# Two attention layers and feed-forwards on one core: two scratch tiles for the masked maxima, one pool of eight PSUM banks, and the order set anew

## The chip, the core and the metric

The kernel runs on one core of a Trainium2 chip. The core has a matrix engine (TensorE; the profile splits it into PE, the matmuls, and PEld, the loads of their weights), VectorE (DVE), ScalarE (ACT), GpSimd (POOL), and queues that issue DMAs (SP's for most of them, ACT's for one kind). The engines run side by side, each takes its own instructions in the order in which they stand, and they wait for each other by semaphores. TensorE writes its results to PSUM, which has eight banks of 512 fp32 values per partition. The metric is device time in microseconds (us) of one launch; the time of a kernel is the median of its runs.

## The reference

Two layers, each of attention A and feed-forward B with a residual and a layer norm, over 2,048 rows of 512 values. Attention has 32 heads of 16 values and takes the rows in 4 segments of 512. Each segment attends causally to itself, reads a memory matrix M that the earlier segments left, and adds to it.

```python
for s in range(4):
    logits = einsum("bhqd,bhkd->bhqk", qs, ks) * scale + mask     # mask: -1e9 above the diagonal
    a_dot  = einsum("bhqk,bhkd->bhqd", softmax(logits), vs)
    a_mem  = einsum("bhld,bhde->bhle", phi(qs), M) / (einsum("bhld,bhd->bhl", phi(qs), z) + 1e-6)
    outs.append(g * a_mem + (1 - g) * a_dot)                      # g = sigmoid(beta), per head
    M, z = M + einsum("bhld,bhle->bhde", phi(ks), vs), z + sum(phi(ks))
x = x + concat(outs) @ wo
x = x + (silu(ln(x) @ w_gate) * (ln(x) @ w_up)) @ w_down          # F = 1792
```

## The kernel before, in words

**Units.** Attention of a layer is cut into 32 units (64 in both layers): 4 segments, 4 groups of 8 heads, and 2 halves of 4 heads each. For every unit the kernel needs the row maxima of the masked logits before it can take exponentials. So each unit has two passes over its scores:

- *Maxima* (`mx_units`): for each of 4 heads, PE fills three banks named pmx (L545): two query tiles in one bank with 256 columns each, then one of 384 columns, then one of 512. DVE goes over each of the four query tiles with one instruction (L552) that adds the mask `amask`, takes the maximum into an accumulator and writes the masked values, which nobody reads, to a scratch tile `junk`. The widths are 128, 256, 384 and 512. In the profile that is CUSTOM_DVE_ANT_0, followed by DVE_READ_ACCUMULATOR2_ANT, which puts the maximum into the tile `mx`; in the order both read ISA. After the four heads PE transposes `mx` (L561), ACT negates it into `nm` (L563), and a DMA from ACT's queue (L564) lays it into a row of the query tile `cq` (in profile and order a tile s), so that the maximum is subtracted by the matmul itself.
- *Scores* (`at_units`): PE fills banks named plt with the transposed scores (L597, two matmuls of 256 columns each, ten tiles per unit), ACT takes exponentials (L603), POOL zeroes what is above the diagonal (L607), and PE multiplies with V into the bank ppv (L624). DVE then transposes the result and divides it: L641, L642, L643, L645, and L658 for every second unit.

Beside the units run the projections of Q, K, V and the output (`mm3`, L283), three products of high and low fp32r halves each; layer norms (L354 to L379); the memory's read and update (L678, L694, L706); and DMAs that lay q and k out by head through DRAM scratch (L493, L494, then `load3`, L518 and L525, into `cq` and `ck`).

**Feed-forward.** Seven chunks of 256 columns; the first is computed directly (`up`, L1005), the rest by `strassen` (L1035) with seven products in place of eight; `down` (L1079) multiplies back, and DVE adds into the residual (L1084).

**Banks.** Every use of PSUM names its bank: plt_0 to plt_2, pmx_0 and pmx_1, ppv, and two called pj, handed out as they become free, for projections and all else. The feed-forward uses the same names.

**Order.** No order is written by hand. Each instruction is an `Op` with an engine, an estimated cost, a priority and its dependences. `issue` (L149) runs through planned time: each engine takes, of what is ready, the instruction of lowest priority value. `LAT` (L43) holds the assumed delays from one engine to the next, `DRAIN` (L40) the change between kinds of matmul. The priorities come from tables: `OFF` for attention (per layer and kind of work), `PRE` for the start, `EP`, `PAIR`, `STEP` and others for the feed-forward. The order in which `issue` takes them is the order in which they stand on the engines, so a wrong estimate shows as a wait on the chip. What waits for what is found anew when the program is built: an instruction that writes a tile waits for those that wrote or read it, on its own engine too.

Of the kernel before, what the change touches and what calls it, by code (L numbers as in the profile page):

```python
# [30 lines left out]
FIN = 17.556  # L31
WQ1 = -21.562
TA, TF = 15.0, 16.7
OFF = ({'qe': (-9.529, 6.646), 'at': (2.962, 3.706), 'mx': (-19.475, -0.147), 'lf': (1.981, -1.419), 'mr': (3.909, 3.093), 'mu': (-9.872, 0.779), 'wo': (3.44, 3.68), 'qk': (5.846, -0.589), 'v': (-0.011, 4.09), 'lp': (17.308, 14.505)},
       {'qe': (10.232, -1.73), 'at': (1.453, 2.403), 'mx': (0.085, 1.514), 'lf': (6.063, -10.056), 'mr': (1.198, 0.041), 'mu': (3.833, -8.363), 'wo': (4.307, -7.535), 'qk': (4.0, -2.887), 'v': (-1.622, 5.91), 'lp': (-0.044, 3.023)})
PRE = {'w1': -20.101, 'w2': 0.722, 'w3': -15.68, 'c': 15.68, 'mb': 7.879, 'lv': 17.87, 'lo': 8.433, 'gate': 15.128, 'v': 10.65, 'dv': 2.669, 'qk1': -14.13, 'mx': 1.541}
EP = {'w': -5.238, 'wn': 8.96, 'ln': -1.878, 'dn': -2.694, 'up': -2.148}
POOL_W = ""
TABLE = 1.28
DRAIN = {("full", "cols"): 0.2, ("cols", "full"): 0.15}  # L40
# [6 lines left out]
    pool=dict(pool=0.14, dve=0.09, pe=0.19, act=0.14, sp=0.07),  # L47
    sp=dict(act=1.2, dve=1.2, pe=1.2, pool=1.2, sp=1.2),
# [3 lines left out]
class Buf:  # L52
    def __init__(self, prog, pool, tag, shape, dtype):
        self.prog, self.pool, self.tag, self.shape, self.dtype = prog, pool, tag, shape, dtype
        self.ops, self.left = [], 0
        self.w, self.r = {}, {}
        self.tile = None
        self.slot = None
        self.prev = None
        if tag not in prog.shared:  # L60
            self.prev = prog.last.get(tag)
            prog.last[tag] = self
# [6 lines left out]
class Op:  # L69
    __slots__ = ("table", "mode", "post", "eng", "cost", "lat", "fn", "prio", "bufs", "succ", "deps", "ready", "need", "wait", "index")  # L70

    def __init__(self, eng, cost, lat, fn, prio, bufs):
        self.eng, self.cost, self.lat, self.fn, self.prio, self.bufs = eng, cost, lat, fn, prio, bufs
        self.mode, self.table, self.post = None, None, 0.0
        self.succ, self.deps, self.ready, self.need, self.wait = [], set(), 0.0, None, 0


class Program:
# [19 lines left out]
    def op(self, eng, cost, fn, reads=(), writes=(), lat=0.0):  # L98
# [38 lines left out]
        for b in touch:  # L137
            assert b.tag in self.shared or self.last[b.tag] is b, f"{b.tag} was given to another buffer"
            b.ops.append(o)
            b.left += 1  # L140
            if b.tag in self.shared:
                o.need = b
# [6 lines left out]
    def issue(self):  # L149
        for b in {id(b): b for o in self.ops for b in o.bufs if b.tag in self.shared}.values():  # L150
# [15 lines left out]
        held = {tag: [] for tag in self.shared}  # L166
        for o in self.ops:
# [3 lines left out]
        while done < len(self.ops):  # L171
            best = None
            for e in engs:
                f, n = fut[e], now[e]
                while True:
# [3 lines left out]
                    if n:  # L179
                        o = n[0][2]  # L180
                        b = o.need
                        if b is not None and b.slot is None:
                            if not free[b.tag]:
                                heapq.heappop(n)
                                held[b.tag].append(o)
                                continue
                            fr = min(free[b.tag])
                            if fr[0] > t[e] + 1e-9:
                                heapq.heappop(n)
                                o.ready = fr[0]  # L190
# [18 lines left out]
            b = o.need  # L209
            if b is not None and b.slot is None:  # L210
                fr = min(free[b.tag])
                free[b.tag].remove(fr)
                b.slot = fr[1]
# [17 lines left out]
            for b in o.bufs:  # L231
                b.left -= 1
                if b.left == 0 and b.slot is not None:
                    free[b.tag].append((end + 0.25, b.slot))
                    for w in held[b.tag]:
# [11 lines left out]
def infini_swiglu(ctx: ExitStack, tc: tile.TileContext, x, wq, wk, wv, wo, beta, wg, wu, wd, out,  # L247
# [8 lines left out]
    P = Program({"pj": 2})  # L256
# [5 lines left out]
    def bank(tag, ring=1):  # L262
        return P.buf(psum, tag, [128, 512], F32, ring)
# [33 lines left out]
    mhalf = sb("mhalf", [128, 1])  # L297
    amask = sb("amask", [128, 512], BF16)
# [98 lines left out]
    def attention(lay, x_in, x_out, slots, T, hook):  # L397
# [134 lines left out]
        def mx_units(u):  # L532
# [4 lines left out]
            def head(p, j):  # L537
                def f():
                    for grp in ((0, 1), (2,), (3,)):
# [9 lines left out]
                        for a, qt in enumerate(grp):  # L549
                            w = 128 * (qt + 1)  # L550
                            junk = sb("junk", [128, 512], BF16)
                            dve(w, lambda a=a, qt=qt, w=w, ps=ps, junk=junk: nc.vector.tensor_tensor_reduce(  # L552
# [186 lines left out]
        if lay == 0:  # L739
# [14 lines left out]
            for t in range(4):  # L754
                ln_fin(0, t, ("plt_0", "plt_1", "plt_2", "ppv")[t])
# [17 lines left out]
        qk_proj(0, 0, "q", "pj" if lay else "pmx_0")  # L773
        qk_proj(0, 0, "k", "pj" if lay else "pmx_1")
# [5 lines left out]
        for t in range(4):  # L780
            at(PRE["v"] + PRE["dv"] * t)
            v_proj(0, t, "pj" if lay else ("plt_0", "plt_1", "plt_2", "ppv")[t])
# [52 lines left out]
    def ffn(base, x_in, x_out, slots, T):  # L835
# [159 lines left out]
        def up(b, fi, ht, early):  # L995
            res = []
            for nm in "gu":
                ps = bank("pj" if early else ("plt_0", "plt_1", "plt_2", "ppv")[nup[0] % 4])
# [18 lines left out]
        def strassen(c, nm, m):  # L1017
# [3 lines left out]
            PX, PY, PZ = [bank(t) for t in (("plt_0", "plt_1", "plt_2") if nm == "g" else ("ppv", "pmx_0", "pmx_1"))]  # L1021
# [214 lines left out]
```

## Time and profile before

| what | value |
|---|---|
| median of 3 runs | 1925.59 us (1921.84 to 1928.22) |
| the profiled execution | 1928.79 us |
| its span, first to last instruction | 1927.1 us |
| mean granted TensorE clock in it | 0.998 |
| DMA | 206.14 MB, 107 GB/s on average |

The span falls into the start (some 48 us), attention of layer 1 (to about 500 us), its feed-forward (to about 1000), attention of layer 2 (to about 1470) and its feed-forward.

How to read a row of the groups: line, engine, operation, what is written <- what is read, the shape, xcount, then after the first bar busy us in total and mean ns of one, then after the second the engine's idle time just before these instructions and who ended it. In a list of waits: who waited <- for whom: us in total, times, longest us. In a timeline: start, duration, engine, line, operation, and in brackets the idle time before it. In a table of windows: the window, its length, busy us of PE, PEld, DVE, ACT and POOL with their instructions, the clock, DMA share and GB/s. PE's ends are modelled, since its matmuls overlap in the array.

### The profile page before, as it was taken

To read this page: it belongs to the slowest core of one execution; us is meant where nothing else is said; L and a number is where in the kernel's file an instruction comes from. 1 tells how busy PE (TensorE), PEld (TensorE's weight loads), DVE (VectorE), ACT (ScalarE), POOL (GpSimd) and SP (SyncE) were. 2 spreads that over 40 slices of the span, in tenths; PEclk is the share of its full clock that TensorE was granted. 3 is DMA by queue.
4 is the path that set the end of the run, shared out by engine and by line. 5 is a ranking of instruction groups with operands and counts; after the bars stand their busy time and mean duration, and the time that the engine had idled before them with its cause. 6 is when DMAs were issued, how large, how long until landed. Compare 5 with 4: busy or idle time off the path is not lost. (4 is left out here: it accounts for less than half of the span.)

```text
span 1927.1 us, 33037 instructions
## 1 busy us (share of the span) xinstructions
PE 1848.0 (96%) x11360; PEld 1448.9 (75%) x11360; DVE 1433.0 (74%) x3834; ACT 884.1 (46%) x1633; POOL 910.1 (47%) x1186
## 2 busy tenths in 40 slices
PE   6899999999999999999999999999999999999999
PEld 5677777776777877788777777777767788877887
DVE  5778778788786669766867768777797856696656
ACT  4455555555634333334435545555455334333331
POOL 5333444434546453746533335443355365546461
PEclk9999999999999999999999999999999999999999
DMA  7534534457131123111364344363561321221121
GB/s 236 137 84 134 147 116 149 127 153 208 39 134 55 44 77 99 55 55 55 105 212 120 102 138 127 101 178 106 161 179 37 132 66 43 84 77 56 44 60 44
DMA packets 126968, 206.14 MB, mean 107 GB/s; under 512 B 14160, under 2 KB 52048, under 8 KB 126800
## 3 DMA queue, kind: packets, MB, share of 16 engines
q1 hardware_dynamic: 124752, 203.49, 35.7%
q8 instruction: 91, 1.49, 0.3%
q10 hardware_dynamic: 2048, 0.53, 0.1%
q14 instruction: 77, 0.63, 0.1%
HBM read 136.34 MB, written 67.11 MB: 106 GB/s over the span
## 5 line engine op out<-in xcount | busy, mean ns | idle before, releaser
L552 DVE CUSTOM_DVE_ANT_0 junk<-pmx,amask 128x128 bf16<-128x128 f32 (+3 forms) x1024 | 495.5, 484 | 98.4 <-PE pmx L545 43.4
L283 PE MATMUL pj<-s,s 128*128 128x512 f32 x1416 | 476.1, 404 | 3.5 <-DVE raw L989 1.4
L1079 PE MATMUL pj<-s,vt 128*128 128x512 f32 x1296 | 405.9, 397 | 3.6 <-DVE s L1084 2.7
L603 ACT ACTIVATE s<-plt 128x512 f32<-128x512 f32 x448 | 255.9, 604 | 202.2 <-PE plt L597 181.9
L1035 PE MATMUL plt<-s,s 128*128 128x512 f32 x1008 | 320.6, 395 | 8.7 <-ACT s L970 4.0
L545 PE MATMUL pmx<-ck,s 127*128 127x256 f32 (+2 forms) x1024 | 301.4, 344 | 20.2 <-DVE mx L552 12.9
L1079 PEld LDWEIGHTS pj<-s,vt 128*128 128x128 f32 x1296 | 242.8, 188 | 67.0 <-DVE s L1084 5.8
L283 PEld LDWEIGHTS pj<-s,s 128*128 128x128 f32 x1416 | 258.8, 189 | 41.5 <-DVE raw L989 2.3
L597 PE MATMUL plt<-s,ck 128*128 128x256 f32 x1280 | 249.3, 288 | 15.0 <-DMA s<-nm 13.7
L1084 DVE TENSOR_TENSOR s<-s,pj 128x512 f32<-128x512 f32 x224 | 152.3, 684 | 141.3 <-PE pj L1079 139.0
L597 PEld LDWEIGHTS plt<-s,ck 128*128 128x128 f32 x1280 | 220.5, 190 | 47.8 <-DMA s<-nm 19.2
L1035 PE MATMUL pmx<-s,s 128*128 128x512 f32 x720 | 242.8, 395 | 0.0
L607 POOL TENSOR_SCALAR_AFFINE_SELECT s<-s 128x512 f32<-128x512 f32 x192 | 129.7, 676 | 233.1 <-ACT s L603 231.8
L1035 PEld LDWEIGHTS plt<-s,s 128*128 128x128 f32 x1008 | 189.2, 188 | 57.2 <-ACT s L970 6.8
L545 PEld LDWEIGHTS pmx<-ck,s 127*128 127x128 f32 x1024 | 177.9, 189 | 71.7 <-DVE mx L552 19.3
L1035 PEld LDWEIGHTS pmx<-s,s 128*128 128x128 f32 x720 | 135.1, 188 | 31.2
L902 POOL TENSOR_TENSOR s<-mem,s 128x512 fp32r<-128x512 f32 x96 | 128.9, 1349 | 0.7 <-ACT s L901 0.7
L1035 PE MATMUL ppv<-s,s 128*128 128x512 f32 x288 | 113.6, 397 | 2.8 <-ACT s L901 2.8
L624 PE MATMUL ppv<-s,vt 128*32 128x384 f32 (+3 forms) x1536 | 115.7, 419 | 0.0
L909 POOL COPY turn<-vt 128x1 f32<-128x1 f32 x20 | 3.7, 185 | 234.0 <-DVE vt L992 234.0
L479 POOL TENSOR_SCALAR s<-raw 128x512 fp32r<-128x512 f32 x64 | 40.6, 634 | 140.3 <-ACT raw L478 137.7
L624 PEld LDWEIGHTS ppv<-s,vt 128*32 128x32 f32 x1536 | 43.4, 109 | 65.1 <-issue 50.5
(201 smaller groups left out, 2981.2 us busy)
## 6 DMA issues: line engine op xcount, KB each, us to landing
s<-scrq SPq DMA_DIRECT2D x128, 192.0 KB, 3.5
ck<-scrk SPq DMA_DIRECT2D x128, 192.0 KB, 4.4
scrq<-s SPq DMA_DIRECT2D x32, 512.0 KB, 4.2
scrk<-s SPq DMA_DIRECT2D x32, 512.0 KB, 3.6
scrq<-s SPq DMA_DIRECT2D x32, 256.0 KB, 2.9
scrk<-s SPq DMA_DIRECT2D x32, 256.0 KB, 2.3
xin<-xmid SPq DMA_DIRECT2D x32, 256.0 KB, 2.7
s<-xmid SPq DMA_DIRECT2D x32, 256.0 KB, 5.4
```

The costliest lines, as they stand in the source:

```text
L283: pe(n, passes, lambda: nc.tensor.matmul(view(ps.ap), lhsT=av(a.ap), rhs=bv(b.ap), start=start, stop=stop), [(a, rk[0]), (b, rk[1])], [ps])
L479: gp(0.59, lambda: nc.gpsimd.tensor_scalar(out=nat.ap[:, a, 0, :], in0=raw.ap, scalar1=1.0, scalar2=0.0, op0=OP.mult, op1=OP.add), [raw], ...
L545: nc.tensor.matmul(ps.ap[:, a * 256:a * 256 + nk], lhsT=cq.ap[0:127, 2 * j + p, qt * 128:(qt + 1) * 128], rhs=ck.ap[0:127, p, 0:nk], start ...
L552: dve(w, lambda a=a, qt=qt, w=w, ps=ps, junk=junk: nc.vector.tensor_tensor_reduce(out=junk.ap[:, :w], in0=ps.ap[:, a * 256:a * 256 + w], i ...
L597: nc.tensor.matmul(ps.ap[:, 256 * p:256 * p + 256], lhsT=ck.ap[:, p, kt * 128:kt * 128 + 128], rhs=cq.ap.rearrange("r (j p) c -> r p j c", ...
L603: act(512, lambda: nc.scalar.activation(view().rearrange("p x i c -> p (x i c)"), ps.ap, AF.Exp, scale=SCALE), [ps], [(Pb, key)], table="exp")
L607: gp(0.593, lambda: nc.gpsimd.affine_select(out=view()[:, 0], in_=view()[:, 0], pattern=[[0, 4], [1, 128]], compare_op=OP.is_ge, fill=0.0, ...
L624: nc.tensor.matmul(ps.ap[32 * i:32 * i + 32, qt * 128:(qt + k) * 128], lhsT=vt.ap[:, kt, VW * hd:VW * hd + 32], rhs=view(k=k)[:, :, idx], ...
L902: gp(n / 400, lambda hi=hi, lo=lo, src=src: nc.gpsimd.tensor_sub(lo(), src(), hi().bitcast(F32)), [read, (wt, (o0, 0))], [(wt, (o0, 1))])
L1035: pe(512, 1, lambda i=i, kc=kc, x=x, buf=buf, view=view: nc.tensor.matmul(ps.ap, lhsT=w.ap[:, o, i, kc], rhs=view(buf.ap, kc), start=(x == 0),
L1079: pe(512, 1, lambda i=i, j=j, fi=fi, x=x, ps=ps, wt=wt, cs=cs: nc.tensor.matmul(ps.ap, lhsT=ht.ap[:, 0:2048].rearrange("p (f a c) -> p f a ...
L1084: dve(512, lambda ps=ps, t=t: nc.vector.tensor_add(xb.ap[:, t, :], xb.ap[:, t, :], ps.ap), [ps, (xb, t)], [(xb, t)])
```

## The change

1. **Two scratch tiles.** `junk` becomes two lasting tiles, junk_0 of 384 and junk_1 of 512 columns; query tiles 0 and 2 write the first, 1 and 3 the second. Each write has a key of its own, so the planner sees no dependence between two maxima. The built program still orders two writers of one tile, so a maximum now waits for the maximum before the last.
2. **One pool of banks.** All eight banks belong to one pool "ps". A use asks for any free bank, under a cap for its class: 3 each for pj, plt, pmx and ppv, 6 for the feed-forward (ff) and 6 for the start (st). In the feed-forward the old names remain as an order of uses, without a fixed bank.
3. **The planner's numbers.** The assumed delays are smaller (PE to ACT 0.20 for 0.29, ACT to PE 0.17 for 0.39, DVE to DVE 0.13 for 0.19), that of a DMA larger (1.9 for 1.2), and all tables of priorities are new. `nm` has one buffer instead of two.

The instructions are the same in kind and number; their order and their banks are not.

```diff
+CAP = {'pj': 3, 'plt': 3, 'pmx': 3, 'ppv': 3, 'ff': 6, 'st': 6}
-WOT = ("pmx_0", "pmx_1", "pj", "pj")
+WOT = ("st", "st", "pj", "pj")
-PAIR, STEP, WAT, TAT = 15.838, 2.488, -12.222, (-12.051, 7.528)
+PAIR, STEP, WAT, TAT = 11.852, 7.441, 15.217, (16.363, 16.627)
...
-    pe=dict(pe=0.01, act=0.29, dve=0.29, sp=0.27),
-    act=dict(act=0.32, dve=0.19, pe=0.39, pool=0.29, sp=0.22),
-    dve=dict(dve=0.19, act=0.19, pe=0.36, pool=0.23, sp=0.17),
...
+    pe=dict(pe=0.01, act=0.2, dve=0.2, pool=0.26, sp=0.19),
+    act=dict(act=0.22, dve=0.13, pe=0.17, pool=0.19, sp=0.15),
+    dve=dict(dve=0.13, act=0.12, pe=0.2, pool=0.17, sp=0.12),
...
-                        b = o.need
-                        if b is not None and b.slot is None:
-                            if not free[b.tag]:
+                        new = [b for b in o.need if b.slot is None]
+                        if new:
+                            tag = new[0].tag
+                            fr = sorted(free[tag])[:len(new)]
+                            if len(fr) < len(new) or not all(turn[b.cls] for b in new):
...
-    P = Program({"pj": 2})
+    P = Program({"ps": 8})
...
     def bank(tag, ring=1):
-        return P.buf(psum, tag, [128, 512], F32, ring)
+        b = P.buf(psum, "ps", [128, 512], F32)
+        b.cls = tag if tag in CAP else "ff"
+        if b.cls == "ff":
+            b.prev = P.last.get(tag)
+            P.last[tag] = b
+        return b
...
+    junks = [sb(f"junk_{i}", [128, 384 + 128 * i], BF16) for i in range(2)]
...
-                            junk = sb("junk", [128, 512], BF16)
-                            dve(w, lambda a=a, qt=qt, w=w, ps=ps, junk=junk: nc.vector.tensor_tensor_reduce(
+                            dve(w, lambda a=a, qt=qt, w=w, ps=ps, junk=junks[qt % 2]: nc.vector.tensor_tensor_reduce(
...
-                                [(ps, a), amask], [junk, (mx, (qt, p, j))])
+                                [(ps, a), amask], [(junks[qt % 2], (lay, u, p, j, qt)), (mx, (qt, p, j))])
...
-                ps, nm = bank("pj"), sb("nm", [16, 128], F32R, ring=2)
+                ps, nm = bank("pj"), sb("nm", [16, 128], F32R)
```

What this makes of the order, at two places. First DVE, where the seventh unit of layer 1 begins its maxima (tile mx_1465 before, mx_1383 now; a read-out of the accumulator is a row that names mx alone; tt, r and Y are the output chain of an earlier unit). Before:

```order
L641 STREAM_TRANSPOSE tt_1397<-ppv 128x512
L552 ISA junk,mx_1265<-pmx_1390,amask 128x512 [waits DVE_49,PE_49]
L552 ISA mx_1265 128x1
L642 RECIPROCAL r_1415<-tt_1397 128x16 [waits DVE_49]
L552 ISA junk,mx_1265<-pmx_1394,amask 128x128 [waits DVE_49,PE_49]
L552 ISA mx_1265 128x1
L643 TENSOR_SCALAR r_1415<-r_1415,gnot 128x16 [waits DVE_49]
L552 ISA junk,mx_1265<-pmx_1394,amask 128x256 [waits DVE_49]
L552 ISA mx_1265 128x1
L645 TENSOR_TENSOR Y<-tt_1397,r_1415 128x16x16 [waits DVE_49]
```

The same place now:

```order
L653 STREAM_TRANSPOSE tt_1337<-ps_1296 128x512
L654 RECIPROCAL r_1345<-tt_1337 128x16 [waits DVE_49]
L655 TENSOR_SCALAR r_1345<-r_1345,gnot 128x16 [waits DVE_49]
L657 TENSOR_TENSOR Y<-tt_1337,r_1345 128x16x16 [waits DVE_49]
L670 STREAM_TRANSPOSE of<-Y 128x512 [waits DVE_49,Pool_49]
L564 ISA junk_439,mx_1383<-ps_1374,amask 128x128 [waits PE_49]
L564 ISA mx_1383 128x1
L564 ISA junk_445,mx_1383<-ps_1374,amask 128x256
L564 ISA mx_1383 128x1
L564 ISA junk_439,mx_1383<-ps_1377,amask 128x384 [waits DVE_49,PE_49]
L564 ISA mx_1383 128x1
```

Before, each step of the chain and a maximum take turns. Now the chain stands in a row, and the maxima stand in a row behind it, on two tiles in turn. Over the whole program 863 of the 1,024 maxima stand right behind a read-out, where 536 did.

Second PE, behind the transpose that closes the maxima of the ninth unit of layer 1 (s_269 and ck_292 are that unit's query and key tiles before, s_232 and ck_251 now; those with ck_98 and ck_90 are the tenth unit's). Before:

```order
L561 MATMUL pj_2036<-ident,mx_1853 16x128
L678 MATMUL pj_2040<-mb_223,phiq_1868 128x136
L545 MATMUL pmx_2048<-ck_98,s_67 128x512
L678 MATMUL pj_2040<-mb_223,phiq_1868 128x136
L678 MATMUL pj_2053<-mb_223,phiq_1868 128x136
L545 MATMUL pmx_2061<-ck_98,s_67 128x256 x2
L678 MATMUL pj_2053<-mb_223,phiq_1868 128x136
L545 MATMUL pmx_2072<-ck_98,s_67 128x384
L545 MATMUL pmx_2081<-ck_98,s_67 128x512
L597 MATMUL plt_2087<-s_269,ck_292 128x256 x2
```

The same place now, the first rows:

```order
L573 MATMUL ps_1853<-ident,mx_1738 16x128
L295 MATMUL ps_1857<-s_1034,s_109 128x512
L609 MATMUL ps_1861<-s_211,ck_222 128x256 x2
L295 MATMUL ps_1857<-s_1034,s_109 128x512
L609 MATMUL ps_1870<-s_211,ck_222 128x256 x2
L295 MATMUL ps_1857<-s_1034,s_109 128x512
```

Before, the unit's own scores (L597) came ten matmuls after the transpose. Now projections (L295) and the unit before it (s_211, ck_222) come first, and the unit's own scores stand 39 matmuls behind. Over all 64 units the median of that distance goes from 34 to 59 matmuls. In the built program 273 fills of the maxima's banks wait for ACT, and 269 fills of the scores' banks for DVE, where none of either did.

More of the change, by code (lines that the diff above doesn't have):

```diff
@@ L166, in issue @@
         held = {tag: [] for tag in self.shared}
+        turn = {c: [0.0] * n for c, n in CAP.items()}
         for o in self.ops:
@@ L208, in issue @@
             heapq.heappop(n)
[L209 to L213, printed above, removed]
+            for b in o.need:
+                if b.slot is None:
+                    fr = min(free[b.tag])
+                    free[b.tag].remove(fr)
+                    b.slot = fr[1]
+                    turn[b.cls].remove(min(turn[b.cls]))
             for b in o.bufs:
@@ L234, in issue @@
                     free[b.tag].append((end + 0.25, b.slot))
+                    turn[b.cls].append(end + 0.25)
                     for w in held[b.tag]:
@@ L1020, in strassen @@
             (h0, l0), (h1, l1) = XT[2 * m], XT[2 * m + 1]
-            PX, PY, PZ = [bank(t) for t in (("plt_0", "plt_1", "plt_2") if nm == "g" else ("ppv", "pmx_0", "pmx_1"))]
+            PX, PY, PZ = [bank(t) for t in (("plt_0", "plt_1", "plt_2") if nm == "g" else ("ppv_0", "pmx_0", "pmx_1"))]
             C, V = {}, {}
```

43 lines of the change are left out of this document (22 added, 21 removed).

## The prediction

> **What bounds the kernel now.** I read the page's busy shares first, then the stages, then who waits for whom, and last single waits in the timeline. First the shares of the whole span:
>
> ```profile
> span 1927.1 us, 33037 instructions
> PE 1848.0 (96%) x11360; PEld 1448.9 (75%) x11360; DVE 1433.0 (74%) x3834; ACT 884.1 (46%) x1633; POOL 910.1 (47%) x1186
> ```
>
> TensorE (PE) is the bound. By this row it is idle for 79.1 us, and no faster neighbour can give back more than what PE loses by waiting. The windows cut the span into start, attention and feed-forward of the two layers; columns are the window, its length, and each engine's busy time with its instructions:
>
> ```profile
> 0.00:48.00 48.00, 32.38 (x130) 25.29 (x130) 28.23 (x76) 22.50 (x39) 28.47 (x50) 1.00 0.73 236
> 48.00:480.00 432.00, 414.70 (x3376) 321.84 (x3376) 346.87 (x1272) 230.11 (x451) 179.28 (x273) 1.00 0.49 140
> 560.00:960.00 400.00, 392.83 (x1700) 315.06 (x1700) 285.14 (x453) 154.76 (x270) 212.85 (x240) 1.00 0.23 71
> 1040.00:1440.00 400.00, 382.31 (x3100) 295.39 (x3100) 309.64 (x1142) 212.57 (x413) 163.82 (x251) 1.00 0.49 137
> 1520.00:1927.10 407.10, 398.31 (x1724) 319.07 (x1722) 280.51 (x435) 146.85 (x257) 199.31 (x217) 1.00 0.20 61
> ```
>
> The two feed-forward windows (560 and 1520) lose 7.2 and 8.8 us. The two attention windows lose 17.3 and 17.7, and there VectorE (DVE) is busy 346.87 of 432 us, 80%. So the second engine matters in attention, and only there. Who ends PE's waits, longest first:
>
> ```profile
> PE plt L597 <- DMA s<-nm: 13.7, 14, 2.3
> PE pmx L545 <- DVE mx L552: 12.9, 29, 0.8
> PE plt L374 <- ACT xn L363: 12.3, 1, 12.3
> PE pmx L545 <- DMA ck<-scrk: 4.6, 6, 2.0
> ```
>
> The 12.3 is the first matmul of the program. The other two large ones belong to one chain: the scores for the row maxima (L545) wait for a bank that the maxima (L552) hold, and the final scores (L597) wait for the negated maxima, which come last of all through a transpose, a copy and a DMA. Two such waits in the timeline:
>
> ```profile
> 157.46 0.27 PE L561 MATMUL pj<-ident,mx 128*16 128x128 f32 x1
> ...
> 159.35 0.44 PE L545 MATMUL pmx<-ck,s 127*128 127x384 f32 x1
> 160.41 0.47 PE L545 MATMUL pmx<-ck,s 127*128 127x512 f32 x1 [0.62 <-DVE mx L552]
> 161.27 0.51 PE L597 MATMUL plt<-s,ck 128*128 128x256 f32 x2 [0.39 <-DMA s<-nm]
> ```
>
> The idle column says 0.62 and 0.39. But from start to start there are 1.06 and 0.86 us. Back to back, a 512-column matmul takes 0.23 us (48.00 us hold 209 of them in the row below), and I take three quarters of that for 384 columns. The two waits therefore cost 0.89 and 0.63, half as much again as printed, because a matmul's modelled end hides the first part of a gap.
>
> ```profile
> 816.00:864.00 48.00, 48.00 (x209) 38.75 (x208) 28.19 (x44) 16.08 (x29) 26.72 (x29) 1.00 0.20 60
> ```
>
> **The change part by part.** *Two scratch tiles.* What a maximum costs now shows in DVE's own timeline:
>
> ```profile
> 300.45 0.08 DVE L552 DVE_READ_ACCUMULATOR2_ANT mx<- 128x1 f32 x1
> 300.68 0.29 DVE L552 CUSTOM_DVE_ANT_0 junk<-pmx,amask 128x128 bf16<-128x128 f32 x1
> 300.89 0.08 DVE L552 DVE_READ_ACCUMULATOR2_ANT mx<- 128x1 f32 x1
> 301.01 0.42 DVE L552 CUSTOM_DVE_ANT_0 junk<-pmx,amask 128x256 bf16<-128x256 f32 x1
> 301.36 0.08 DVE L552 DVE_READ_ACCUMULATOR2_ANT mx<- 128x1 f32 x1
> 301.36 0.68 DVE L728 TENSOR_TENSOR xin<-xin,pj 128x512 f32<-128x512 f32 x1
> 301.96 0.55 DVE L552 CUSTOM_DVE_ANT_0 junk<-pmx,amask 128x384 bf16<-128x384 f32 x1
> 302.44 0.08 DVE L552 DVE_READ_ACCUMULATOR2_ANT mx<- 128x1 f32 x1
> ```
>
> A maximum that writes the tile of the one before it waits for that one's read-out to end: 300.45 + 0.08 to 300.68 is 0.15 us of gap, and 301.01 comes 0.04 after 300.97 (here it waits for DVE alone, not for PE too). The addition at 301.36 waits for neither, and starts together with the read-out. The maximum at 301.96, with an addition in between, starts 0.08 before that addition ends. So a freed maximum starts 0.08 us before its predecessor's end, not 0.04 to 0.15 after it: it gains 0.12 or 0.23. The trace has no freed maximum right behind a read-out, so the bounds are 0 and 0.23; I take the gain whole, since both neighbours (addition behind read-out, maximum behind addition) show it. In the old order 536 of 1,024 maxima stand right behind a read-out, 145 of them of 256 columns: 391 x 0.23 + 145 x 0.12 = 107 us of DVE time.
>
> *What the order gives back on DVE.* The output chain (transpose, reciprocal, scale, multiply) had maxima between its steps; now its steps stand in a row, about 160 more direct waits over 64 units. At 0.12 each (0.04 gap plus 0.08 overlap lost, as in the rows above) that is 19 us. DVE's net gain is 88 us, 1.4 per unit. All of it is beside PE's work: its worth is only what PE now waits for.
>
> *PE's waits for maxima (L545).* Here are both halves of PE, the matmul queue and the weight loads that run ahead and meet the semaphore first:
>
> ```profile
> PEld pmx L545 <- DVE mx L552: 19.3, 46, 1.1
> PEld plt L597 <- DMA s<-nm: 19.2, 15, 2.6
> PEld pmx L545 <- issue: 10.6, 29, 0.5
> ```
>
> Lower bound 12.9 (PE's own idle, none of the hidden part), upper 1.5 x 20.2 + 10.6 = 41 (all of PE's idle before L545 by the group below, with its hidden half and the unnamed part). I take 28, near 19.3 + 10.6, because DVE gets 1.4 us per unit of slack and a third bank may be filled ahead.
>
> *PE's waits for the negated maxima (L597).* The chain to be covered runs from the transpose at 157.46 to 161.27 in the rows above, 3.8 us, most of it the DMA's landing:
>
> ```profile
> DMA to landing us min/median/max: 1.8/3.1/7.0
> ```
>
> From the transpose to the first final scores of the same unit the new order puts a median of 59 matmuls where 34 stood. At attention's mean of 0.13 us (432 us for 3,376) that is 7.7 in place of 4.4 us, against a chain of 3.8. Nearly all units are then covered; the first one, 9 matmuls where 14 stood, still waits some 2 us. Bounds: 0 and 1.5 x 13.7 = 21; I take 17. The single nm buffer makes ACT's copy wait for the DMA before it, with the exponentials of L603 queued behind; that DMA lies a unit back (48 us hold about three), so nothing.
>
> *Everything else in the order and the banks.* The groups show what is left of PE's idle time, and what DVE idles before the maxima:
>
> ```profile
> L552 DVE CUSTOM_DVE_ANT_0 junk<-pmx,amask 128x128 bf16<-128x128 f32 (+3 forms) x1024 | 495.5, 484 | 98.4 <-PE pmx L545 43.4 <-PE plt L597 0.8 <-DVE mx L552 0.7
> L545 PE MATMUL pmx<-ck,s 127*128 127x256 f32 (+2 forms) x1024 | 301.4, 344 | 20.2 <-DVE mx L552 12.9 <-DMA ck<-scrk 4.6 <-DVE rm L682 0.6
> L597 PE MATMUL plt<-s,ck 128*128 128x256 f32 x1280 | 249.3, 288 | 15.0 <-DMA s<-nm 13.7 <-ACT s L603 0.9
> L1035 PE MATMUL plt<-s,s 128*128 128x512 f32 x1008 | 320.6, 395 | 8.7 <-ACT s L970 4.0 <-DVE s L971 3.8 <-POOL s L902 0.4
> ```
>
> 79.1 - 12.3 - 12.9 - 13.7 = 40 us, 60 with the hidden part, spread over stage borders (L1035's 8.7 among them) and projections. The matmuls, the DMAs, their sizes and their number do not change. The new latencies (0.20 for PE to ACT in place of 0.29, 0.17 in place of 0.39 back) only shift where the plan thinks room is. I take a gain of 10, with -15 (a border that falls worse) and +30 as bounds. The start loads x two DMAs earlier, and PE then meets the same wait for the first ck: nothing.
>
> Sum: 28 + 17 + 10 = 55 us. The profiled execution took 1928.8 (span 1927.1 and 1.7 around it), 3.2 over the median of the runs, 1925.6. 1928.8 - 55 = 1873.8, and on the median's scale 1870.6: **1871 us**, 2.8% less.
>
> **The rivals.** *A. Slower: the maxima stay serial.* The new order relies on them: 863 of them now stand right behind a read-out, 327 more than before. If 0.15 of gap and 0.08 of lost overlap remain, DVE gets 327 x 0.23 = 75 us of work more, not 107 less, and the chain's 19 on top. Of the present 107 about 28 reach PE, so of these 94 some 25 would, and with the other terms gone the time is 1951. DVE breaks even where each of the 863 costs 88 / 863 = 0.10 us over a free start, that is 0.02 us after its predecessor's end; from there on the change is slower on DVE. The Trainium skill, page "VectorE: DVE Perf Modes", section "The DRAIN you can't avoid", says so: the next operation cannot start until the pipe is empty, and leaving out the semaphore gains nothing. The addition at 301.36, which starts with the read-out, speaks against that here, though of no maximum behind a read-out is it shown.
>
> *B. Also slower or level: the shared pool makes PE wait for another engine.* PE takes its queue in order, so a bank that is late holds all behind it. In the old order no fill of L545 waits for ACT and none of L597 for DVE; in the new one 273 and 269 do. If each came 0.1 us late, 54 us and the gain would be gone (1925); from there on it is slower. Against it: the group rows show ACT half idle, and an eviction of 0.6 us lies well inside a turn of three banks.
>
> *C. The waits move to the loads.* A ck load lands late already now (4.6 us of PE's waits above), and its median is long:
>
> ```profile
> ck<-scrk SPq DMA_DIRECT2D x128, 192.0 KB, 4.4
> ```
>
> The SP queue issues the same loads; if PE runs ahead of it, they take back half of the gain: 1898.
>
> *D. More.* If the stage borders tighten as well (30 in place of 10) and both attention terms reach their upper bounds, 41 + 21 + 30 = 92: 1834.
>
> **How the numbers follow.** Forecast 0.45 (its own range 1852 to 1890), C 0.22, D 0.16, A 0.07, B 0.10. Range: 1840 to 1912 leaves out A, half of B and a part of D, about 0.2. A difference under 0.3%, about 6 us, is what a measurement of this kernel cannot tell from none. Slower: A and a little of B, 0.09. Same: 0.04 of B and the end of C, 0.05. Faster: 0.86.
>
> **What would show it.** In the profile after: maxima that start with the read-out before them, so that DVE's idle time before the maxima, now 98.4, halves; fewer us on "PE pmx <- DVE mx" and "PE plt <- DMA s<-nm"; PE's busy time unchanged within the hidden part; attention windows some 22 us shorter in each layer, and feed-forward windows as long as now. It is wrong if read-outs still precede maxima by 0.15 (A), if PE's list of waits is led by many short waits for ACT before the scores and for DVE before the final scores (B), or by DMA (C).

## The result, and the profile after

| | median | range | runs |
|---|---|---|---|
| before | 1923.71 us | 1921.01 to 1928.22 | 4 |
| after | 1877.15 us | 1875.80 to 1878.99 | 4 |

The ratio is 0.9743, with a 95% interval from 0.972 to 0.9766: 46.6 us less, where 55 were forecast. The profiled execution took 1878.99 us, its span 1877.2.

The busy shares of the whole span, from the top of the page of after:

```profile
span 1877.2 us, 33021 instructions
PE 1825.3 (97%) x11360; PEld 1450.6 (77%) x11360; DVE 1407.5 (75%) x3834; ACT 873.1 (47%) x1629; POOL 918.9 (49%) x1186
```

PE is still the bound, with the same 11,360 matmuls. Its idle time fell from 79.1 to 51.9 us, by 27.2, and its busy time from 1848.0 to 1825.3, by 22.7, though no matmul went. The second figure is the part of the waits that a modelled matmul end hides. So here the hidden part is 0.83 of the printed one, not the half that the prediction took from two single waits.

Only the ends of the matmuls are modelled, so their starts give the whole loss. For each pair of neighbouring kinds of matmul, the usual distance from start to start (the 30th percentile in both traces together) is taken off; what a distance has above it is counted as lost before the later matmul. The usual distances add up to 1680 us in both kernels, so the 50 us of span are lost time. This is an estimate; with the median in place of the percentile, no difference between the two columns changes by more than 1 us:

| PE's lost time, us | before | after |
|---|---|---|
| before the maxima's fills | 48.4 | 16.1 |
| before the final scores | 36.9 | 28.5 |
| before the transpose of `mx` | 2.1 | 7.6 |
| before the first matmul | 12.3 | 9.8 |
| all else (71 of it in both before the products with V) | 147.0 | 134.8 |

Where a fill waited for a maximum, it lost 24.5 us before and 0.6 after.

The stages (window, length, then busy us of PE, PEld, DVE, ACT and POOL with their instructions, clock, DMA share, GB/s):

```profile
48.00:480.00 432.00, 424.64 (x3539) 335.54 (x3538) 343.62 (x1320) 244.97 (x481) 189.47 (x286) 1.00 0.48 140
560.00:960.00 400.00, 390.73 (x1698) 314.31 (x1697) 284.42 (x470) 150.85 (x263) 223.21 (x247) 0.99 0.27 79
1040.00:1400.00 360.00, 353.52 (x2940) 279.58 (x2938) 282.38 (x1079) 197.90 (x390) 153.60 (x236) 1.00 0.51 145
1480.00:1877.20 397.20, 390.18 (x1688) 312.96 (x1686) 274.67 (x422) 145.19 (x253) 198.98 (x217) 1.00 0.19 58
```

In the first attention window 3,539 matmuls fit where 3,376 did, and PE loses 7.4 us instead of 17.3; in the second it loses 6.5 of 360 us, before 17.7 of 400. The first feed-forward window holds 1,698 matmuls against 1,700, with 9.3 us lost against 7.2. So the gain lies for the most part in attention, as forecast, and the inside of the feed-forward runs at its old pace. One kind of instruction did change in number: ACT loads its tables 8 times instead of 12, 1.28 us each, nearly all of them around the borders between attention and feed-forward. What this is worth to PE was not tried.

Who ends PE's waits now (who waited <- for whom: us, times, longest):

```profile
PE ps L387 <- ACT xn L376: 9.8, 1, 9.8
PE ps L558 <- DMA ck<-scrk: 4.9, 4, 2.8
PE ps L573 <- DVE mx L564: 4.7, 9, 1.7
PE ps L1047 <- ACT s L982: 4.6, 4, 2.6
PE ps L609 <- DMA s<-nm: 4.5, 4, 1.7
```

The lines have moved: the maxima's fills are now L558 (L545 before), the maxima L564 (L552), their transpose L573 (L561), the final scores L609 (L597). "Fills wait for maxima", 12.9 us before, is gone from the head of the list, and "final scores wait for the negated maxima" fell from 13.7 to 4.5. One entry is new: the transpose of `mx` waits for the last maximum itself. It is small here; the first experiment shows what stands behind it. The groups:

```profile
L564 DVE CUSTOM_DVE_ANT_0 junk<-ps,amask 128x128 bf16<-128x128 f32 (+3 forms) x1024 | 433.5, 484 | 46.5 <-PE ps L558 45.1
...
L558 PE MATMUL ps<-ck,s 127*128 127x256 f32 (+2 forms) x1024 | 276.6, 334 | 5.7 <-DMA ck<-scrk 4.9
L609 PE MATMUL ps<-s,ck 128*128 128x256 f32 x1280 | 250.6, 287 | 6.4 <-DMA s<-nm 4.5
```

DVE's idle time before the maxima went from 98.4 to 46.5 us, and of that PE ends 45.1 (43.4 before): what went is the waiting of DVE for itself. Busy time fell from 495.5 to 433.5, since a maximum now runs beside the read-out before it. DVE's own timeline shows both, one head of four maxima in layer 1:

```profile
258.76 0.08 DVE L564 DVE_READ_ACCUMULATOR2_ANT mx<- 128x1 f32 x1
258.76 0.29 DVE L564 CUSTOM_DVE_ANT_0 junk<-ps,amask 128x128 bf16<-128x128 f32 x1
258.97 0.08 DVE L564 DVE_READ_ACCUMULATOR2_ANT mx<- 128x1 f32 x1
258.97 0.42 DVE L564 CUSTOM_DVE_ANT_0 junk<-ps,amask 128x256 bf16<-128x256 f32 x1
...
259.31 0.55 DVE L564 CUSTOM_DVE_ANT_0 junk<-ps,amask 128x384 bf16<-128x384 f32 x1
...
259.79 0.69 DVE L564 CUSTOM_DVE_ANT_0 junk<-ps,amask 128x512 bf16<-128x512 f32 x1
...
260.40 0.29 DVE L564 CUSTOM_DVE_ANT_0 junk<-ps,amask 128x128 bf16<-128x128 f32 x1
```

Each maximum starts at the moment the read-out before it starts. Over all 863 that stand behind a read-out, the median start is 83 ns before the read-out's end; before the change it was 144 ns after it (391 maxima), or 35 ns where the maximum waited for DVE alone (145). A head takes 258.76 to 260.40, 1.64 us.

### The profile page after: what moved, and what is told of

It is laid out like the page before. It is cut to its first block, busy times and chain, and to the rows that moved or that the text cites. A ratio compares the mean times of both kernels' runs of the same rounds, so it can differ in the third digit from the quotient of the medians.

```text
span 1877.2 us, 33021 instructions
## 1 busy us (share of the span) xinstructions
PE 1825.3 (97%) x11360; PEld 1450.6 (77%) x11360; DVE 1407.5 (75%) x3834; ACT 873.1 (47%) x1629; POOL 918.9 (49%) x1186
## 4 chain that ended last, share of the span: by engine, by line
PE 48%; DVE 7%; issue 2%; DMA 2%; POOL 1%; ACT 1%; SPq 0%; DVEq 0%; POOLq 0%; ACTq 0%
PE ps L1047 18%; PE ps L1091 10%; PE ps L295 7%; PE ps L636 3%; PE ps L558 3%; PE ps L609 3%; DVE junk L564 2%; DMA s<-nm 1%; PE ps L1017 1%; DVE tt L961 1%; DVE s L983 1%; DVE s L1096 1%; PE ps L387 1%; DVE mx L564 0%; DVE of L961 0%
## 5 line engine op out<-in xcount | busy, mean ns | idle before, releaser
L1047 PE MATMUL ps<-s,s 128*128 128x512 f32 x2016 | 547.3, 396 | 9.5 <-ACT s L982 4.6
L295 PE MATMUL ps<-s,s 128*128 128x512 f32 x1536 | 526.2, 407 | 2.7 <-ACT s L451 1.2
L564 DVE CUSTOM_DVE_ANT_0 junk<-ps,amask 128x128 bf16<-128x128 f32 (+3 forms) x1024 | 433.5, 484 | 46.5 <-PE ps L558 45.1
L1047 PEld LDWEIGHTS ps<-s,s 128*128 128x128 f32 x2016 | 376.7, 188 | 106.0 <-ACT s L982 6.7
L1091 PE MATMUL ps<-s,vt 128*128 128x512 f32 x1296 | 378.0, 397 | 2.2 <-ACT vt L1003 2.2
L295 PEld LDWEIGHTS ps<-s,s 128*128 128x128 f32 x1536 | 287.2, 191 | 51.6 <-issue 6.1
L615 ACT ACTIVATE s<-ps 128x512 f32<-128x512 f32 x448 | 253.9, 609 | 108.5 <-PE ps L609 97.2
L1091 PEld LDWEIGHTS ps<-s,vt 128*128 128x128 f32 x1296 | 245.2, 189 | 58.6 <-ACT vt L1003 2.6
L558 PE MATMUL ps<-ck,s 127*128 127x256 f32 (+2 forms) x1024 | 276.6, 334 | 5.7 <-DMA ck<-scrk 4.9
L609 PE MATMUL ps<-s,ck 128*128 128x256 f32 x1280 | 250.6, 287 | 6.4 <-DMA s<-nm 4.5
L609 PEld LDWEIGHTS ps<-s,ck 128*128 128x128 f32 x1280 | 221.3, 189 | 38.3 <-issue 4.9
L558 PEld LDWEIGHTS ps<-ck,s 127*128 127x128 f32 x1024 | 177.6, 189 | 28.8 <-issue 6.4
L1017 PE MATMUL ps<-s,s 128*128 128x512 f32 x384 | 123.9, 400 | 0.9 <-ACT s L391 0.9
L636 PEld LDWEIGHTS ps<-s,vt 128*32 128x32 f32 x1536 | 43.3, 109 | 64.1 <-issue 46.2
L615 ACT ACTIVATE pc<-ps 128x512 f32<-128x512 f32 x128 | 78.7, 615 | 19.9 <-PE ps L609 19.3
```

The lines of the kernel that those rows point to most:

```text
L295: pe(n, passes, lambda: nc.tensor.matmul(view(ps.ap), lhsT=av(a.ap), rhs=bv(b.ap), start=start, stop=stop), [(a, rk[0]), (b, rk[1])], [ps])
L558: nc.tensor.matmul(ps.ap[:, a * 256:a * 256 + nk], lhsT=cq.ap[0:127, 2 * j + p, qt * 128:(qt + 1) * 128], rhs=ck.ap[0:127, p, 0:nk], start ...
L564: dve(w, lambda a=a, qt=qt, w=w, ps=ps, junk=junks[qt % 2]: nc.vector.tensor_tensor_reduce(out=junk.ap[:, :w], in0=ps.ap[:, a * 256:a * 25 ...
L609: nc.tensor.matmul(ps.ap[:, 256 * p:256 * p + 256], lhsT=ck.ap[:, p, kt * 128:kt * 128 + 128], rhs=cq.ap.rearrange("r (j p) c -> r p j c", ...
L615: act(512, lambda: nc.scalar.activation(view().rearrange("p x i c -> p (x i c)"), ps.ap, AF.Exp, scale=SCALE), [ps], [(Pb, key)], table="exp")
L636: nc.tensor.matmul(ps.ap[32 * i:32 * i + 32, qt * 128:(qt + k) * 128], lhsT=vt.ap[:, kt, VW * hd:VW * hd + 32], rhs=view(k=k)[:, :, idx], ...
```

## The experiments

The theory of the prediction (P): the free start of the maxima gives DVE time, and a part of that reaches PE. Its rivals in the runs: the order and the pool carry the gain by themselves (T), or tiles, pool and order are worth something only together (I).

**1 and 2. One tile in the new order, two tiles in the old.** The order stays as it is on every engine; only the tile behind the writes changes. The first:

```diff
-    junks = [sb(f"junk_{i}", [128, 384 + 128 * i], BF16) for i in range(2)]
+    junks = [sb("junk", [128, 512], BF16)] * 2
```

> The changed kernel, in its own order on every engine and with its own banks, but both scratch tiles are one tile of 512 columns again, so each maximum waits for the read-out before it. Theory P (the prediction's: the free start of the maxima is what PE gets back): the 863 maxima that stand behind a read-out lose about 0.2 us each again, some 170 us of DVE time; of the 107 us priced in the old order 28 reached PE, so about 45 of these do: 1922, and up to the 1951 of rival A; DVE's idle time before the maxima from 46 to over 100 us, and PE waits for maxima again. Theory T (the new order and the pool of banks carry the gain, the serial maxima lie beside PE's work): 1877 to 1890, with PE's waits for maxima under 5 us.

Measured: 2019.58 us, ratio to before 1.0487 [1.0469, 1.0504]. That is 142 us over the change, and far over both theories. The group of the maxima, and PE's list of waits:

```profile
L564 DVE CUSTOM_DVE_ANT_0 junk<-ps,amask 128x128 bf16<-128x128 f32 (+3 forms) x1024 | 501.2, 489 | 138.2 <-PE ps L558 39.8
```

```profile
PE ps L573 <- DVE mx L564: 41.7, 36, 2.8
PE ps L558 <- DVE mx L564: 14.5, 51, 0.9
PE ps L609 <- DVE mx L564: 11.3, 34, 0.8
```

DVE pays what was worked out: 68 us more busy time and 92 us more idle time, 160 together where the expectation had 170. But 142 of these 160 us reach the end, nine tenths, where the prediction had let a quarter through. From start to start, PE loses 44 us more before the transpose (L573), 41 before the fills and 29 before the final scores. The transpose is where single waits are longest. The same run's timeline:

```profile
298.36 0.08 DVE L564 DVE_READ_ACCUMULATOR2_ANT mx<- 128x1 f32 x1
298.61 0.42 DVE L564 CUSTOM_DVE_ANT_0 junk<-ps,amask 128x256 bf16<-128x256 f32 x1 [0.17 <-DVE mx L564]
...
299.19 0.56 DVE L564 CUSTOM_DVE_ANT_0 junk<-ps,amask 128x384 bf16<-128x384 f32 x1
...
299.90 0.69 DVE L564 CUSTOM_DVE_ANT_0 junk<-ps,amask 128x512 bf16<-128x512 f32 x1
300.52 0.08 DVE L564 DVE_READ_ACCUMULATOR2_ANT mx<- 128x1 f32 x1
300.66 0.38 PE L573 MATMUL ps<-ident,mx 128*16 128x128 f32 x1 [1.99 <-DVE mx L564]
```

From the 384-wide maximum to the 512-wide one there are 0.71 us here and 0.48 in the changed kernel, 0.23 more, as priced. The transpose stands in PE's queue where the plan expects the last maximum to be done. When the maxima of a unit come late, PE stands still there, here for 1.99 us, and all matmuls behind wait with it.

The second run turns it round:

```diff
+    JK = [pool.tile([128, 384 + 128 * i], BF16, name=f"junk_{i}", tag=f"junk_{i}") for i in range(2)]
...
                             junk = sb("junk", [128, 512], BF16)
+                            junk.tile = JK[qt % 2]
```

> The kernel before, in its own order and with its own fixed banks, but the maxima write two scratch tiles in turn (and nm has one buffer, to make room). 536 maxima stand right behind a read-out and start freely. Theory P: DVE gets 107 us back, PE's waits for maxima (term A, 28 us) go: 1896, between 1883 and 1910; PE's waits for the negated maxima stay near 13 us, since the distances in PE's queue do not change. Theory T (order and banks carry the gain): 1915 to 1924, with PE's waits for maxima still over 8 us.

Measured: 1919.09 us against 1925.06, ratio 0.9961 [0.9941, 0.9981]: 6 us, 4 to 11 by the interval. Theory P falls in its size: its 28 us are not there, and the time and the 8.8 us of waits for maxima are theory T's. In the groups and the waits of this run (the maxima are L555, their fills L547):

```profile
L555 DVE CUSTOM_DVE_ANT_0 junk<-pmx,amask 128x128 bf16<-128x128 f32 (+3 forms) x1024 | 472.2, 479 | 103.7 <-PE pmx L547 100.9
```

```profile
PE plt L601 <- DMA s<-nm: 12.4, 11, 2.1
PE plt L376 <- ACT xn L365: 11.6, 1, 11.6
PE pmx L547 <- DVE mx L555: 8.8, 21, 1.1
```

The free start works here too, and DVE's idle time does not fall: it was 98.4 with 43.4 ended by PE, and is 103.7 with 100.9 ended by PE. DVE now waits for the fills, because PE takes them at the same places of its queue as before. From start to start, PE loses 39.1 us before the fills where it lost 48.4, so 9 us came of it there. In an order that stands still, the faster engine here mostly waits longer.

**6 and 9. The wait for the negated maxima.** Their DMA goes to a DRAM scratch, so that no final scores wait for it, in the old order with two tiles and in the new order:

```diff
-                    cq.ap[127:128].bitcast(F32).rearrange("o x (t c) -> o (x t) c", t=4),
+                    (cq.ap[127:128].bitcast(F32) if u < NB else dram.tile(
+                        [1, 4, 512], F32, name=f"nx{lay}_{u}", tag=f"nx{lay}_{u}")).rearrange("o x (t c) -> o (x t) c", t=4),
```

> The old order with two tiles (the second run's kernel), and the negated maxima of all units but the first three of each layer go to a DRAM scratch, so that no final scores wait for them (the subtraction then uses older maxima: part of the computation is changed). Theory P: terms A and B together, 28 + 17 us: 1880, between 1865 and 1890. Rival (in an order that stands still, a wait that goes is met by the next one): the 12.4 us of that wait and half as much again hidden, taken from 1919: 1900, or 1910 if part of it reappears as waits for maxima or for ACT.

> The changed kernel in its own order, but the negated maxima of all units but the first three of each layer go to a DRAM scratch, so that no final scores wait for them (the subtraction uses older maxima: part of the computation is changed). It tells what is left of term B, which was 17 us in the old order. Prediction's term B (the longer distance covers the chain in nearly all units): 1870 to 1875. If the longer distance only moved the wait: 1865 or less.

Measured: 1901.96 us in the old order (ratio 0.9878 [0.9853, 0.9903]), 17.1 less than the second run. That it is term B's 17 us to the digit is luck, since the two intervals leave some 6 us either way; the rival's 1900 fits as well, theory P's 1880 does not. In the new order 1875.03 (ratio 0.9733 [0.9719, 0.9748]), 2 us under the change and not to be told from it. One wait for the negated maxima is left in each run, among the first three units of a layer:

```profile
PE plt L602 <- DMA s<-nm: 1.6, 1, 1.6
PE ps L610 <- DMA s<-nm: 1.7, 1, 1.7
```

So the longer distance (59 matmuls for 34) did cover the chain in nearly all units, and about 15 us of the gain are this term.

**3, 4, 11, 5, 12 and 7. The parts with an order of their own.** Each part gets tables of priorities that were searched for it, with the plan's own end as the measure, always with the new delays. An example of what differs, from the fourth run:

```diff
-FIN = 17.556
-WQ1 = -21.562
+FIN = 5.535
+WQ1 = -45.919
```

> The kernel before (fixed banks, one scratch tile, two nm buffers) with the new assumed delays, and tables of priorities of its own that were searched anew for just this kernel: the change's third part alone. Theory N (the numbers carry the gain: a better order was to be had all along): 1895 or less. Theory I (tiles and pool have to come together, the order only uses them): 1905 to 1925, with PE's waits for maxima and for the negated maxima still 15 us or more together.

> Fixed banks as before, but two scratch tiles that the planner knows of (and one nm buffer), the new delays, and tables searched anew for this kernel: the change without the pool. Theory P (the prediction's: the free start of the maxima and an order that uses it are the gain, the pool is worth little): 1875 to 1890. Theory I (the maxima need the third bank too): 1900 to 1920, no better than the kernel with one tile beside it, DVE idle before the maxima waiting for PE.

> Fixed banks, two tiles, new delays, as in the run that gave 1947, with a second set of tables from a search of its own that ended level by its plan. It tells how far two such searches lie apart on the chip. If the 50 us between fixed banks and pool are the structure: 1930 to 1960. If they are the luck of a search: 1915 or less.

> The changed kernel with its pool and its delays, but one scratch tile, the planner told that each maximum costs DVE 0.16 us more, and tables searched anew for this kernel: the change without the second tile. If the pool is what counts: 1895 or less. Theory P and theory I: the serial maxima are on the path once the order is tight, 1910 or more; DVE's idle time before the maxima over 100 us.

> Pool and one tile, as in the run that gave 1944, with the planner told 0.23 us for each serial maximum in place of 0.16 (what the traces show: 144 ns after the read-out instead of 83 ns before it) and tables searched anew. If the second tile is needed whatever the order: 1915 to 1950. If the earlier run was only planned on a wrong price: 1905 or less.

> The changed kernel (pool, two tiles, new delays), but with other tables of priorities: searched anew by the plan alone, from the tables of before, in the way of the three kernels with a part of the change. It separates the structure from the one set of tables that came with it. Theory I (tiles and pool together make room for a better order, whatever the tables): 1875 to 1905, at least 35 us under the kernel with fixed banks and two tiles (1947). Theory S (the gain lies in that one set of tables): 1925 to 1950, like the other three.

| orders searched for the kernel | one tile | two tiles |
|---|---|---|
| fixed banks | 1956.74 | 1946.97 and 1952.64 |
| pool of eight | 1943.79 and 1955.48 | 1897.10 |

The three theories of one carrier (N, P, pool alone) find no support: none of the parts alone comes below the kernel before (ratios from 1.0090 [1.0061, 1.0118] to 1.0164 [1.0138, 1.0190]), while both together, with tables of a search of their own, give 1897.10 (ratio 0.9849 [0.9833, 0.9864]). Tiles alone are worth 4 to 10 us, the pool alone 1 to 13, both together 60. Two searches of the same kernel lie 6 and 12 us apart, so the 47 us or more between the last cell and the others are the structure rather than the luck of a search, though the last cell has only one. The searches ended near each other and near the change's own tables (scores of layer 2: 1.266 and 1.885 in the last cell, 1.308 and 1.885 with fixed banks and two tiles, 1.287 and 1.907 in the change); only the first cell's lie elsewhere (0.879 and 2.399), so the 4 to 10 and 1 to 13 us are less sure than the 47. The third and fourth run came out 27 us or more slower than any range set for them, the twelfth 5: a search by the plan alone finds worse orders for the chip than the tables that came with the two kernels. Those beat their searched neighbours by some 32 us (before against 1956.74) and 20 us (after against 1897.10). So the cells are compared with each other, not with the kernel before, and a better order with the old banks and tile is not ruled out (theory N). The new delays were never tried without new tables, so what they are worth by themselves is not shown.

What the missing part does shows in where PE loses time from start to start, before the fills and before the final scores (us, from each kernel's trace):

| fills / final scores | one tile | two tiles |
|---|---|---|
| fixed banks | 64.2 / 28.4 | 47.1 / 31.4 and 55.3 / 32.8 |
| pool of eight | 37.4 / 43.3 and 26.2 / 54.7 | 19.9 / 28.0 |

The pool takes the loss from the fills with one tile too, but then the final scores lose more; only with both are the two small. The groups show the same. Fixed banks and two tiles (the fourth run), PE's and DVE's side:

```profile
L552 DVE CUSTOM_DVE_ANT_0 junk<-pmx,amask 128x256 bf16<-128x256 f32 (+3 forms) x1024 | 458.6, 483 | 87.2 <-PE pmx L546 73.4
...
L546 PE MATMUL pmx<-ck,s 127*128 127x256 f32 (+2 forms) x1024 | 306.3, 351 | 14.3 <-DVE mx L552 11.8 <-DMA ck<-scrk 0.3 <-DVE rm L682 0.3
L546 PEld LDWEIGHTS pmx<-ck,s 127*128 127x128 f32 x1024 | 178.4, 189 | 76.9 <-DVE mx L552 25.2 <-PE pmx L546 11.8 <-issue 9.0
```

Both wait for each other: DVE 73.4 us for fills, PE's loads 25.2 us for banks that a maximum still holds. Pool and one tile (the fifth run):

```profile
L567 DVE CUSTOM_DVE_ANT_0 junk<-ps,amask 128x128 bf16<-128x128 f32 (+3 forms) x1024 | 498.9, 487 | 113.4 <-PE ps L561 28.7
```

Here PE ends only 28.7 of DVE's 113.4 us; the rest is DVE behind its own read-outs. Pool and two tiles with the other tables (the seventh run):

```profile
L564 DVE CUSTOM_DVE_ANT_0 junk<-ps,amask 128x128 bf16<-128x128 f32 (+3 forms) x1024 | 436.9, 482 | 50.7 <-PE ps L558 49.7
...
L558 PE MATMUL ps<-ck,s 127*128 127x256 f32 (+2 forms) x1024 | 277.2, 337 | 7.5 <-POOL s L494 2.6 <-DVE mx L564 2.3 <-ACT s L615 0.9
```

Both waits are small, as in the changed kernel.

**8. A cap of two banks for the maxima.**

```diff
-CAP = {'pj': 3, 'plt': 3, 'pmx': 3, 'ppv': 3, 'ff': 6, 'st': 6}
+CAP = {'pj': 3, 'plt': 3, 'pmx': 2, 'ppv': 3, 'ff': 6, 'st': 6}
```

> The changed kernel with the maxima's cap at two banks instead of three, and tables searched on from those of the change. Theory I (the maxima need the third bank, so that PE can fill ahead of DVE): 1900 to 1920, DVE's idle time before the maxima, waiting for PE, up from 45 us. If two do (the pool's worth is with the other uses): 1877 to 1890.

Measured: 1903.54 us (ratio 0.9888 [0.9865, 0.9912]). The time is theory I's, its sign is not:

```profile
L564 DVE CUSTOM_DVE_ANT_0 junk<-ps,amask 128x128 bf16<-128x128 f32 (+3 forms) x1024 | 450.8, 482 | 54.2 <-PE ps L558 48.4
```

DVE waits 48.4 us for fills, hardly more than the 45.1 of the change. Against the change the third bank would be worth 26 us, against the other searched kernel 6. With two banks at most, as with fixed banks, the time is still 43 us under the better kernel with fixed banks and two tiles, and from start to start PE loses 20.7 us before the fills, where that kernel loses 47.1. So the pool's gain is not only the maxima's third bank; which of the other uses (projections, scores, output) carries it was not tried and stays open.

**10. Shorter maxima.**

```diff
-                                out=junk.ap[:, :w], in0=ps.ap[:, a * 256:a * 256 + w], in1=amask.ap[:, 512 - w:],
+                                out=junk.ap[:, :max(128, w // 2)], in0=ps.ap[:, a * 256 + w - max(128, w // 2):a * 256 + w],
+                                in1=amask.ap[:, 512 - max(128, w // 2):],
```

> The changed kernel in its own order, but each maximum runs over half its columns (the last 128, 128, 192 and 256 of 128 to 512), so part of the computation is left out. By the profile of after (684, 551, 419 and 284 ns for the four widths) DVE gets 256 x (0.135 + 0.20 + 0.265) = 154 us back, about what one tile took from it in the first run (there +142 us in time). Theory O (the order was planned for the free start: DVE is just in time, a delay goes to PE almost whole, a gain goes nowhere): 1868 to 1877, and DVE's idle time before the maxima, waiting for PE, grows by over 80 us. Rival (DVE still sets PE's pace in attention): 1840 or less.

Measured: 1870.26 us (ratio 0.9703 [0.9682, 0.9724]), 7 us under the change; theory O. The maxima's group:

```profile
L564 DVE CUSTOM_DVE_ANT_0 junk<-ps,amask 128x128 bf16<-128x128 f32 (+2 forms) x1024 | 306.5, 338 | 119.4 <-PE ps L558 111.0
```

127 us of DVE's work are gone (154 were expected), and its waiting for PE is 111.0 us where it was 45.1: 66 more, not the over 80 that the theory had named. The time is inside its range. Together with the first run: 160 us more on DVE cost 142, 127 less bring 7. DVE is not the bound, and has little slack.

## Why the prediction was right, and where not

The forecast of 1871 us lay 6 us under the result, inside its own range of 1852 to 1890. The sum came out, and so, nearly, did the places where PE loses less. For the largest term, what brings it about was wrong.

*The free start.* Right as taken: 83 ns before the end of the read-out (0.08 in the prediction), and 0.23 us for each freed maximum. The Trainium skill, page "VectorE: DVE Perf Modes", section "The DRAIN you can't avoid", which the prediction set beside rival A, says that a semaphore between operations costs nothing extra; for these pairs leaving out the wait gains 144 + 83 ns. The prediction left out that the same section excepts a next operation that is not held. Another section of the page, "Two Vector instructions with no wait between them", says that a held instruction starts only when every earlier Vector instruction has finished; the freed maxima start 83 ns before that, so they were not held. A's price was wrong as well, and by more: where the gap does remain, the new order takes 2020 us, not 1951. The prediction had carried over the old order's share (28 of 107 us reach PE) to an order that is built on the free start, and there nine tenths do.

*Term A, 28 us (fills waiting for maxima).* Right in place and near in size, wrong in its cause. PE loses 32 us less before the fills, 24 of them where a maximum was waited for; 5.5 come back before the transpose. The step that failed is the one from DVE's gain to PE's waits: the prediction paid for the term with the free start, 1.4 us of DVE per unit, and the free start alone gives 6 us (9 before the fills; the waits for a maximum go from 24.5 to 15.5). It read a wait that ends on DVE as one that a faster DVE takes away. But the fills stand at fixed places of PE's queue, so most of what DVE gains becomes its own waiting for PE (100.9 us for 43.4), and most of PE's printed 12.9 us stays (8.8). The rest of the term comes with the pool and an order made for it (19.9 us lost before the fills in the seventh run, 47.1 in the fourth). Of the pool the prediction had one clause, the third bank that may be filled ahead, and the run with a cap of two shows that most of the gain there does not need it (20.7 us).

*Term B, 17 us (the wait for the negated maxima).* Right in size and reason: 17.1 us in the old order, 2 left in the new one, where four such waits remain, the longest 1.7 us. Before the final scores PE loses only 8 us less in all, since other waits grew there: their loads now wait 3.9 us for maxima and 2.9 for ACT. The single nm buffer cost nothing to speak of: ACT's copy waited for the DMA once.

```profile
  DMA s<-nm: 3.6, 1
```

*Term C, 10 us (everything else).* By place it was a little small: with the start, the other places give some 15 us. By parts it looks otherwise: 46.6 less 6 (tiles in the old order) and 15 (term B) leaves about 26 us, just under the upper bound of 30, and this is the room that pool and tiles give the order together, 60 us between searched orders. Most of it shows before the fills, at the place of term A. Since the parts work only together, neither split is the only one. "The start: nothing" missed a little: PE's first wait fell from 12.3 to 9.8.

*Rivals B, C, D.* The shared pool brings many more waits in the program and few in time: before the maxima's fills PE and its loads wait 1.9, 1.4 and 1.1 us in all for ACT's work on three kinds of tiles, and before the final scores PE waits 0.6 us for DVE and its loads 3.9. The ck loads cost 4.9 us instead of 4.6. The three upper bounds of D did not come together.

## What to carry to other kernels

Before you price a wait by the engine that ends it, ask whether the waiting engine's queue would come any earlier: here, with the order as it was, the faster neighbour mostly waited instead, and the gain came only with an order (and the buffers) that uses it. An order planned for a fast step turns the step's slack into speed, and then a late step can cost almost its whole length (142 of 160 us here); undo such a part by itself and you measure the new order's fragility, not the part's worth. Measure parts as a table of two by two, each cell with an order of its own.

## What the runs showed of the hardware

- A maximum that writes another tile starts with the read-out of the one before it (both at 258.76 in the timeline above), not only beside its end. With the same tile the gap is 35 ns where it waits for DVE alone, and 144 ns where it waits for DVE and PE; the second wait costs some 0.11 us by itself. The Trainium skill, page "Perfetto Trace Analysis", section "Identifying Dependency Chains", says that an instruction which waits for several engines may get a semaphore instruction of its own ahead of it; in the trace of before all 391 maxima with the long gap have one, and none of the 145 with the short gap.
- PE's waits are nearly half hidden in its busy time: of 49.9 us of span that went, 27.2 were printed as idle and 22.7 as busy, while the usual distances from start to start add up to 1680 us in both kernels.
